# Seven block sums of a Strassen-like second layer, issued one at a time over two steps

## The chip, the core and the metric

One core of a Trainium2 chip runs the whole kernel. The metric is device time in microseconds (us) of one execution. The kernel before was run three times: 1166.24, 1168.34 and 1169.35 us, median 1168.34 us.

The core's engines run side by side and each takes its own instructions in order: TensorE (PE, matmuls; PEld, the loads of its weights), VectorE (DVE), ScalarE (ACT), GpSimd (POOL), and SyncE (SP), which here only issues DMAs. Matmul results land in PSUM, which has eight banks of 128 x 512 float32; everything else lies in SBUF or in DRAM.

## The reference

Chunked attention is followed by two feed-forward layers on 3072 tokens of width 512, with 2048 hidden columns each:

```python
x = attention(q, k, v, mem_k, mem_v)          # (3072, 512)
h = x @ w_in;  x = relu(h) ** 2 @ w_out       # first layer
h = x @ w_in2; g = h * tanh(softplus(h))      # second layer
return g @ w_out2
```

Input and output are float32.

## The kernel before, in words

Each layer works on blocks of 1024 tokens: blocks 0 to 2 belong to the first layer and blocks 3 to 5 to the second. A block takes eight steps, one for each 256 hidden columns, so step s is step s % 8 of block s // 8. Steps 24 to 47 are the second layer's, and the call `step(48)` holds only the end.

Each matrix product is a 2 x 2 block product in Winograd's form: seven products of blocks and of sums of blocks take the place of eight. Each product is made of float32 split into a rounded part and a rest, so that one product of a 256 x 256 by 256 x 512 block takes six matmuls per 128 output rows: high times high, low weight times high, high weight times low.

A step of the second layer does two things in turn. It computes the hidden columns of step s by seven first products, P1, P6, P5, P2, P7, P4, P3 (`product`, line 478), in PSUM banks 0, 1 and 2 (a, b, c). VectorE forms u2, u3, c22, c21 and c12 from them (lines 744, 763, 765, 771, 776), and ScalarE applies the activation (line 501). Between these products it multiplies the hidden columns of step s - 1 with the output weights by seven second products (`product2`, line 568), which I call n0 to n6. Their places in the step are fixed by `wait_point`: P1 P6 n0 P5 n1 P2 n2 P7 n3 n4 P4 P3 n5 n6. Product n takes the block `PRODUCTS2[n][1]`; before, these are B11, B22, B21, T3, T1, T2, T4. Each has two banks: the pairs 4-5 and 6-7 take turns.

The block's operand g is made by `sums_g` (VectorE, line 519: T3, T1, T2, T4), then cast by ScalarE (line 491), then its rest is found by POOL (line 492).

Each second product is added into an SBUF tile m of 128 x 1024 by VectorE (line 556); in a block's first turn, ScalarE copies it there instead (line 579). The tiles of n0, n1 and n2 have tags named by `spare`, ("xt" or "raw") + 0 to 2; the tiles of n3 and n4, and those of n5 and n6, share one buffer each, y0 and y1. A tile of the same tag may be written only when all readers of the one before it have ended.

After the last step of a block, seven sums of the m tiles give its four output blocks (`combine`): T2+=B11, T3+=T2, T2+=T1, T1+=T3, then T4+=T3, B22+=T2, B21+=B11. Each is one VectorE addition of 128 x 1024 with both operands in SBUF, also at line 556. T1, T4, B22 and B21 are then stored (`store_y`). For blocks 3 and 4, the last results come during the first step of the next block (steps 32 and 40), and the first results of the next block during the step after (33 and 41). `done(i)` is called after product n_i and decides which sums stand there. Before, four sums stand after n5 (T2) of steps 32 and 40, and one after each of n0, n1 and n2 of steps 33 and 41.

The last step's hidden columns (step 47) are not multiplied in Winograd's form but by four plain products in step 48 (`last_unit`, line 607), each of 12 matmuls in two banks, added into T4, B21, T1 and B22 and stored. Block 5's sums are made in step 47, ahead of them.

`rest()` is called after each product; there SP issues one load of weights of the step or the next (lines 243 and 245) and the stores that were put off.

Of the kernel before, what the change touches and what calls it, by code (L numbers as in the profile page):

```python
# [25 lines left out]
NQ = KF // 2  # L26
NSB = NT // (2 * NB)
# [9 lines left out]
A22, A11, A12, S1, S2, S3, S4 = range(7)  # L37
B22, B11, B21, T1, T2, T3, T4, B12 = range(8)
P1, P6, P5, P2, P7, P4, P3 = range(7)
PRODUCTS = [(A11, B11), (S2, T2), (S1, T1), (A12, B21), (S3, T3), (A22, T4), (S4, B22)]  # L40

PRODUCTS2 = [(A11, B11), (S4, B22), (A12, B21), (S3, T3), (S1, T1), (S2, T2), (A22, T4)]
STEPS = 2 * NSB * NQ

OUTPUTS = {T4: (1, 0), B21: (0, 0), T1: (1, 1), B22: (0, 1)}
FIRST2 = NSB * NQ
PSB = NP // NSB
POINTS = 15
# [3 lines left out]
def tile_chunk_attention_moe_moe2(  # L52
# [56 lines left out]
    def where(s):  # L109
        return s // (NSB * NQ), s // NQ, s % NQ  # L110
# [165 lines left out]

    def spare(sb, i):

        return f"{('xt', 'raw')[sb % NSB % 2]}{i % 3}"

    def load_apart(sb, o):
        xt_t[sb, o] = pool.tile([128, 2 * NB], FP32, tag=spare(sb - 1, 2 * o), name="xa")
# [189 lines left out]
    def product(s, o, ps, start, stop):  # L472
        wi, xi = PRODUCTS[o]
        w = w1_t[s]
        order = [(kk, a, 0) for kk in range(2) for a in range(2)] + [(kk, 0, 1) for kk in range(2)]
        for i, (kk, a, c) in enumerate(order):
            f = 256 * wi + 128 * kk
            nc.tensor.matmul(  # L478
                out=ps,
                lhsT=w[:, a, f:f + 128],  # L480
                rhs=x[:, xi, c, kk, :],
                start=start and i == 0,
                stop=stop and i == len(order) - 1,
                skip_group_check=True,
            )
# [3 lines left out]
    def split_g(s, key, r):  # L489
        g = g_t[s, key] = new_g(where(s)[0], key)  # L490
        nc.scalar.copy(out=g[:, 0], in_=r)  # L491
        nc.gpsimd.tensor_tensor(out=g[:, 1], in0=r, in1=g[:, 0].bitcast(FP32), op=ALU.subtract)  # L492
# [56 lines left out]
    pairs = [0]  # L549

    def store_y(sb, i, t, y):
        o = 2 * NB * (sb % NSB) + NB * t
        later(out[2 * i:2 * i + 2, :, o:o + NB].rearrange("d p s -> p d s"), y)

    def add(to, in0, in1, engine=nc.vector):
        engine.tensor_tensor(out=to, in0=in0, in1=in1, op=ALU.add)  # L556
# [24 lines left out]
        m = m_t[sb, blk]  # L581
        add(m, ps, m)

    def combine(sb, blk, store):

        m = {b: m_t[sb, b] for _, b in PRODUCTS2}
        if blk == T2:
            add(m[T2], m[T2], m[B11])
            add(m[T3], m[T3], m[T2])
            add(m[T2], m[T2], m[T1])  # L590
            add(m[T1], m[T1], m[T3])
        else:
            add(m[blk], m[blk], m[{T4: T3, B22: T2, B21: B11}[blk]])
        if store:
            store_y(sb, *OUTPUTS[T1 if blk == T2 else blk], m[T1 if blk == T2 else blk])

    def last_unit(s, n):

        sb = where(s)[1]
        blk = list(OUTPUTS)[n]  # L600
        i, t = OUTPUTS[blk]
        first = (4 + 2 * (pairs[0] % 2), 4 + 2 * ((pairs[0] + 1) % 2), 0, 2)[n]
        w = w2_t[s].rearrange("p c (b f) -> p c b f", b=4)
        order = [(f, a, 0) for f in range(2) for a in range(2)] + [(f, 0, 1) for f in range(2)]
        for d in range(2):
            for e, (f, a, c) in enumerate(order):
                nc.tensor.matmul(  # L607
                    out=bank(first + d),
                    lhsT=w[:, a, (2 + f, f)[i], 128 * d:128 * d + 128],
                    rhs=g_t[s, ((B11, B12), (B21, B22))[f][t]][:, c, :],  # L610
                    start=e == 0,
                    stop=e == len(order) - 1,
                )
        m = m_t[sb, blk]
        add(m, banks[:, first:first + 2], m)
        store_y(sb, i, t, m)
        flush()
# [58 lines left out]
    def step(s):  # L676
        live, prev = s < STEPS, s > 0
        layer, sb, j = where(s) if live else (None, None, None)
        point = [0]

        def rest():
            flush()
            i = point[0]
            if NQ <= s + 1 < STEPS and i % 2 == 0 and i < POINTS - 1:
                stream_w(s + 1, 0, i // 2)
            if FIRST2 <= s < STEPS and i % 2 and i // 2 < (7 if s < STEPS - 1 else 4):
                stream_w(s, 1, i // 2)
            if NQ <= s < FIRST2 and i % 3 == 1 and i < 11:
                stream_w(s, 1, i // 3)
            for w in beside.pop((s, point[0]), []):  # L690
                w()
            point[0] += 1

        def units_of(n):
            for i in n:
                if prev:
                    unit(s - 1, i // 4, i % 4, rest)
                else:
                    rest()

        def multiply2(n):
            if prev:
                product2(s - 1, n, rest)
            else:
                rest()

        flush()
        second = s > FIRST2
        if s == FIRST2:
            more["r"] = pool.tile([128, 2, NB], FP32, tag="val", name="more")  # L710

        def wait_point(n):

            if second:
                for i in ((), (0,), (1,), (2,), (3, 4), (5, 6))[n]:
                    product2(s - 1, i, rest)
                    done(i)
            else:
                units_of(((), (), (0, 1), (), (2, 3, 4), (5, 6, 7))[n])

        def done(i):
            _, sb, j = where(s - 1)
            final = s == STEPS - 1
            if (j == NQ - 1 or final) and PRODUCTS2[i][1] == T2:
                combine(sb, T2, not final)
            if final and PRODUCTS2[i][1] == T4:
                for blk in (T4, B22, B21):
                    combine(sb, blk, False)
            if sb > NSB and j == 0 and i < 3:
                combine(sb - 1, (T4, B22, B21)[i], True)  # L730

        if live:
            a, b, c = bank(0), bank(1), bank(2)
            product(s, P1, a, True, False)
            rest()
            u1 = ring("u", 3, [128, NB], FP32, "u1")
            nc.scalar.copy(out=u1, in_=a)  # L737
            if second:
                sums_g(s - 1, T2)
                split_g(s - 1, T3, r_ff[s - 1, T3])  # L740
            product(s, P6, b, True, False)
            rest()
            u2 = ring("u", 3, [128, NB], FP32, "u2")
            nc.vector.tensor_tensor(out=u2, in0=b, in1=u1, op=ALU.add)
            if second:
                sums_g(s - 1, T4)
                split_g(s - 1, T1, r_ff[s - 1, T1])
            wait_point(1)
            product(s, P5, c, True, False)
            rest()  # L750
            if second:
                split_g(s - 1, T2, r_ff[s - 1, T2])
            wait_point(2)
            product(s, P2, a, False, True)
            rest()
            gate(s, 0, 0, a, new_r(layer))
            if second:
                split_g(s - 1, T4, r_ff[s - 1, T4])
            wait_point(3)
            product(s, P7, b, False, False)  # L760
            rest()
            u3 = ring("u", 3, [128, NB], FP32, "u3")
            nc.vector.tensor_tensor(out=u3, in0=b, in1=u1, op=ALU.add)  # L763
            c22 = new_r(layer)
            nc.vector.tensor_tensor(out=c22, in0=c, in1=u3, op=ALU.add)
            gate(s, 1, 1, c22, c22)
            wait_point(4)
            product(s, P4, b, False, True)
            rest()
            c21 = new_r(layer)  # L770
            nc.vector.tensor_tensor(out=c21, in0=b, in1=u1, op=ALU.add)  # L771
            gate(s, 1, 0, c21, c21)
            product(s, P3, c, False, True)
            rest()
            c12 = new_r(layer)
            nc.vector.tensor_tensor(out=c12, in0=c, in1=u2, op=ALU.add)
            gate(s, 0, 1, c12, c12)
            wait_point(5)
            if layer == 1 and s < STEPS - 1:
                sums_g(s, T3)  # L780
                sums_g(s, T1)
        else:
            for n in range(4):
                last_unit(s - 1, n)
        for i in range(POINTS):
            for w in beside.pop((s, i), []):
                w()
        flush()
        if prev and where(s - 1)[0] == 0 and where(s - 1)[2] == NQ - 1:
            sums_y(where(s - 1)[1])  # L790

    with tc.manual_schedule():
# [77 lines left out]
        for n, e in enumerate(seconds):  # L870
            if n < NQ - 2:
                plan_w(NQ + n, 0, e, "Aa|D|d|RS|s|L||||r|l", lambda e, i: round_w2(e, i, "xt2"), split_w2, "val")
            else:
# [4 lines left out]
                    lambda e, i, hi=hi: round_w2(e, i, hi[i]), split_w2, ("val", "at0")[n % 2],  # L878
# [9 lines left out]
        for sb in range(1, 2 * NSB):  # L888
            s = sb * NQ - 1
# [80 lines left out]
```

## Time and profile before

| | |
|---|---|
| three runs | 1166.24, 1168.34, 1169.35 us |
| the profiled execution | 1169.24 us |
| its span, first to last instruction | 1167.2 us |
| TensorE's mean granted clock | 0.972 of full speed |
| busy: PE, DVE, ACT, POOL | 1079.9, 896.1, 561.5, 430.0 us |

All times are counted from the span's start. A row of a timeline gives the start, the duration, the engine, the source line, the operation, what it writes and reads, and how many like instructions in a row it stands for. Brackets hold the idle time just before and what ended it. A row of 12 matmuls that runs on into the next ends, as printed, 0.16 us behind the next one's start, since the end of a matmul is modelled. Where a wait is put down to "issue", the profile shows no other engine that ended it.

The page's chain of waits puts 56% of the span on TensorE and 11% on VectorE. In the second layer, TensorE's rows follow each other without a gap in most steps; they break where a block ends.

### The profile page before, as it was taken

The page shows a single profiled execution, that of the slowest core. Times are in us where ns is not written, and L with a number is a line of the kernel's source. Part 1 is how long each engine was busy: PE and PEld are TensorE (multiplying, and loading weights), DVE is VectorE, ACT ScalarE, POOL GpSimd, SP SyncE. Part 2 cuts the span into 40 slices and gives each one's busy share as a digit, 9 for nine tenths or more (in the row PEclk, how much of TensorE's full clock was granted, in tenths as well). Part 3 has the DMA queues.
Part 4 walks back from the last instruction along what each step waited for, and adds up shares of the span by engine and source line. Part 5 has one row for each costly group of instructions (what it writes and reads, how often), then busy time and mean ns, then how long its engine had stood idle before and what let it go on. Part 6 is the DMA issues. An engine that isn't in the chain of part 4 may idle for free.

```text
span 1167.2 us, 19779 instructions
## 1 busy us (share of the span) xinstructions
PE 1079.9 (93%) x7478; PEld 881.1 (75%) x7478; DVE 896.1 (77%) x1164; ACT 561.5 (48%) x879; POOL 430.0 (37%) x333
## 2 busy tenths in 40 slices
PE   6869899898799889999999999999989999799997
PEld 5748688776677778887777778888868888578885
DVE  5586879969666655678998677898878988768886
ACT  2467555555454444557565645444354443253331
POOL 2423223232223323223222244555355545245451
PEclk9999899999989889999999999999999999899998
DMA  9556867777998786869999958989997889867531
GB/s 359 231 193 233 293 214 262 260 277 248 384 320 315 263 292 241 280 237 395 342 338 329 362 218 289 314 304 339 345 309 276 303 304 391 277 207 230 161 128 72
DMA packets 192125, 324.94 MB, mean 278 GB/s; under 512 B 13344, under 2 KB 151072, under 8 KB 188192
## 3 DMA queue, kind: packets, MB, share of 16 engines
q1 hardware_dynamic: 192032, 323.69, 78.0%
q8 instruction: 60, 0.98, 0.3%
q14 instruction: 33, 0.27, 0.1%
HBM read 231.62 MB, written 92.01 MB: 277 GB/s over the span
## 4 chain that ended last, share of the span: by engine, by line
PE 56%; DVE 11%; DMA 7%; ACT 4%; issue 3%; SPq 0%; DVEq 0%; ACTq 0%
PE banks L478 26%; PE banks L568 17%; PE banks L533 10%; DMA w_d<-hi 2%; DVE m L556 2%; DVE y L547 1%; PE banks L414 1%; PE banks L607 1%; DMA w1s<-w_d 1%; DVE ty L632 1%; DVE val L152 1%; DVE r L519 1%; ACT r L497 1%; DMA xt<-xt_d 1%; DMA w2s<-w_d 1%
## 5 line engine op out<-in xcount | busy, mean ns | idle before, releaser
L478 PE MATMUL banks<-x,w1s 128*128 128x512 f32 x2016 | 507.8, 399 | 23.5 <-DVE u L763 7.5
L492 POOL TENSOR_TENSOR g<-r,g 128x512 fp32r<-128x512 f32 x206 | 287.3, 1401 | 537.5 <-ACT g L491 442.6
L478 PEld LDWEIGHTS banks<-x,w1s 128*128 128x128 f32 x2016 | 385.8, 193 | 112.5 <-DVE u L763 9.7
L533 PE MATMUL banks<-g,w2s 128*128 128x512 f32 x1152 | 282.4, 395 | 6.8 <-DVE y L547 5.3
L533 PEld LDWEIGHTS banks<-g,w2s 128*128 128x128 f32 x1152 | 217.2, 190 | 57.7 <-DVE y L547 8.2
L568 PE MATMUL banks<-g,w2s 128*128 128x512 f32 x966 | 241.3, 392 | 9.8 <-ACT m L579 7.6
L568 PEld LDWEIGHTS banks<-g,w2s 128*128 128x128 f32 x966 | 181.2, 189 | 52.2 <-ACT m L579 9.7
L556 DVE TENSOR_TENSOR m<-banks,m 128x1024 f32<-128x1024 f32 x144 | 173.6, 1218 | 34.9 <-PE banks L568 26.3
L491 ACT CAST g<-r 128x512 fp32r<-128x512 f32 x206 | 127.0, 621 | 37.5 <-DVE r L519 30.3
L547 DVE TENSOR_TENSOR y<-banks,y 128x512 f32<-128x512 f32 x168 | 112.0, 682 | 39.0 <-PE banks L533 38.9
L492 POOL TENSOR_TENSOR g<-more,g 128x512 fp32r<-128x512 f32 x55 | 79.7, 1453 | 81.0 <-ACT g L491 66.6
L497 ACT ACTIVATE r<-r 128x512 f32<-128x512 f32 x72 | 45.4, 631 | 69.7 <-DVE r L771 50.1
L501 ACT ACTIVATE r<-r 128x512 f32<-128x512 f32 x48 | 30.4, 632 | 71.4 <-DVE r L771 35.9
L211 ACT CAST hi<-val 128x1024 fp32r<-128x1024 f32 (+1 forms) x32 | 30.4, 949 | 69.5 <-DVE val L156 50.5
L498 ACT ACTIVATE r<-r 128x512 f32<-128x512 f32 x96 | 60.7, 632 | 3.1
L152 DVE TENSOR_SCALAR val<-val 128x512 f32<-128x512 f32 x64 | 38.9, 607 | 26.5 <-ACT val L145 26.4
L414 PE MATMUL banks<-pt,v 64*64 64x32 f32 x1536 | 39.9, 262 | 19.4 <-ACT pt L402 19.0
L218 DVE TENSOR_TENSOR val<-val,hi 128x1024 f32<-128x1024 f32 (+1 forms) x32 | 37.2, 1162 | 25.2 <-ACT hi L211 25.0
L414 PEld LDWEIGHTS banks<-pt,v 64*64 64x64 f32 x1536 | 37.0, 185 | 25.7 <-ACT pt L402 24.8
L737 ACT COPY u<-banks 128x512 f32<-128x512 f32 x48 | 28.1, 585 | 52.0 <-PE banks L478 52.0
L384 POOL TENSOR_TENSOR p<-p,sum 128x512 f32<-128x512 f32 x24 | 28.7, 1215 | 63.3 <-DVE sum L381 25.0
L344 PE MATMUL banks<-k,q 64*32 64x64 f32 x1536 | 37.5, 250 | 13.2 <-DMA k<-k_dram 7.1
(71 smaller groups left out, 999.9 us busy)
## 6 DMA issues: line engine op xcount, KB each, us to landing
w1s<-w_d SPq DMA_DIRECT2D x280, 256.0 KB, 5.4
w2s<-w_d SPq DMA_DIRECT2D x229, 256.0 KB, 5.3
raw<-w_dram SPq DMA_DIRECT2D x64, 512.0 KB, 5.0
w_d<-w1s SPq DMA_DIRECT2D x8, 1792.0 KB, 7.5
x<-xs_d SPq DMA_DIRECT2D x14, 1024.0 KB, 10.7
k<-k_dram SPq DMA_DIRECT2D x24, 512.0 KB, 7.0
v<-v_dram SPq DMA_DIRECT2D x24, 512.0 KB, 8.9
xt<-xt_d SPq DMA_DIRECT2D x21, 512.0 KB, 7.3
```

What stands on the lines that cost most here:

```text
L152: nc.vector.tensor_scalar(out=val, in0=val, scalar1=LIMIT, scalar2=-LIMIT * NEGATIVE, op0=ALU.min, op1=ALU.max)
L344: nc.tensor.matmul(out=s4[32 * c:32 * c + 32, j, hp, :], lhsT=q_t[p][r0:r0 + 64, j, hp, 32 * c:32 * c + 32], rhs=k_t[p][r0:r0 + 64, j, hp, ...
L414: nc.tensor.matmul(out=x_ps[par][64 * h2:64 * h2 + 64, o:o + 32], lhsT=v_t[p][j][r0:r0 + 64, h2, a, c, :], rhs=pt_t[p][r0:r0 + 64, h2, j, ...
L478: nc.tensor.matmul(out=ps, lhsT=w[:, a, f:f + 128], rhs=x[:, xi, c, kk, :], start=start and i == 0, stop=stop and i == len(order) - 1, ski ...
L491: nc.scalar.copy(out=g[:, 0], in_=r)
L492: nc.gpsimd.tensor_tensor(out=g[:, 1], in0=r, in1=g[:, 0].bitcast(FP32), op=ALU.subtract)
L497: nc.scalar.activation(out=r, in_=h, func=ACTF.Relu)
L498: nc.scalar.activation(out=r, in_=r, func=ACTF.Square)
L533: nc.tensor.matmul(out=ps, lhsT=w[:, a, blk(f), d % 2 * 128:d % 2 * 128 + 128], rhs=g_t[s, (f, t)][:, c, :], start=i == 0, stop=i == len(o ...
L547: nc.vector.tensor_tensor(out=y, in0=ps, in1=y, op=ALU.add)
L556: engine.tensor_tensor(out=to, in0=in0, in1=in1, op=ALU.add)
L568: nc.tensor.matmul(out=bank(first + d), lhsT=w[:, a, 128 * d:128 * d + 128], rhs=g[:, c, :], start=i == 0, stop=i == 2)
```

## The change

Four things change. `PRODUCTS2` swaps T1 and T2, so n4 is T2 and n5 is T1, and with it the pairs that share a buffer: T3 and T2 in y0, T1 and T4 in y1. The seven sums become a list, `SUMS`, and `done` issues them one by one: T2+=B11 after n4 and T3+=T2 after n5 of the block's last products; T2+=T1 ahead of P6 of the step after; T1+=T3, T4+=T3, B22+=T2 and B21+=B11 after n0, n1, n2 and n3 of it, the last four with a store each. In step 47 the first stands after n4, three after n5 and three after n6. `spare` takes turns from block 3 on: the fifth block's first three tiles are tagged raw and not xt, as the fourth's are. Last, `last_unit` begins in banks 0-1 and 2-3 and then takes the two pairs.

```diff
-PRODUCTS2 = [(A11, B11), (S4, B22), (A12, B21), (S3, T3), (S1, T1), (S2, T2), (A22, T4)]
+PRODUCTS2 = [(A11, B11), (S4, B22), (A12, B21), (S3, T3), (S2, T2), (S1, T1), (A22, T4)]
+SUMS = [(T2, B11), (T3, T2), (T2, T1), (T1, T3), (T4, T3), (B22, T2), (B21, B11)]
...
-        return f"{('xt', 'raw')[sb % NSB % 2]}{i % 3}"
+        return f"{('xt', 'raw')[(sb - NSB) % 2]}{i % 3}"
...
-    def combine(sb, blk, store):
+    def combine(sb, to, other, store=False):
         m = {b: m_t[sb, b] for _, b in PRODUCTS2}
-        if blk == T2:
-            add(m[T2], m[T2], m[B11])
-            add(m[T3], m[T3], m[T2])
-            add(m[T2], m[T2], m[T1])
-            add(m[T1], m[T1], m[T3])
-        else:
-            add(m[blk], m[blk], m[{T4: T3, B22: T2, B21: B11}[blk]])
-        if store:
-            store_y(sb, *OUTPUTS[T1 if blk == T2 else blk], m[T1 if blk == T2 else blk])
+        add(m[to], m[to], m[other])
+        if store and (to, other) in SUMS[3:]:
+            store_y(sb, *OUTPUTS[to], m[to])
...
-        first = (4 + 2 * (pairs[0] % 2), 4 + 2 * ((pairs[0] + 1) % 2), 0, 2)[n]
+        first = (0, 2, 4 + 2 * (pairs[0] % 2), 4 + 2 * ((pairs[0] + 1) % 2))[n]
...
         def done(i):
             _, sb, j = where(s - 1)
-            final = s == STEPS - 1
-            if (j == NQ - 1 or final) and PRODUCTS2[i][1] == T2:
-                combine(sb, T2, not final)
-            if final and PRODUCTS2[i][1] == T4:
-                for blk in (T4, B22, B21):
-                    combine(sb, blk, False)
-            if sb > NSB and j == 0 and i < 3:
-                combine(sb - 1, (T4, B22, B21)[i], True)
+            blk = PRODUCTS2[i][1]
+            if s == STEPS - 1:
+                for n in {T2: (0,), T1: (1, 2, 3), T4: (4, 6, 5)}.get(blk, ()):
+                    combine(sb, *SUMS[n])
+            elif j == NQ - 1:
+                for n in {T2: (0,), T1: (1,)}.get(blk, ()):
+                    combine(sb, *SUMS[n])
+            elif sb > NSB and j == 0:
+                for n in {B11: (3,), B22: (4,), B21: (5,), T3: (6,)}.get(blk, ()):
+                    combine(sb - 1, *SUMS[n], store=True)
...
                 split_g(s - 1, T3, r_ff[s - 1, T3])
+                if where(s - 1)[1] > NSB and where(s - 1)[2] == 0:
+                    combine(where(s - 1)[1] - 1, *SUMS[2])
             product(s, P6, b, True, False)
```

The first place is VectorE from n5's addition in step 32 to u3 in step 33. Before, m_6714 is the buffer of T2 and T4, m_6673 that of T3 and T1, and m_6606, m_6625 and m_6649 are B11, B22 and B21:

```order
L556 TENSOR_TENSOR m_6714<-banks_70,m_6714 128x1024
L556 TENSOR_TENSOR m_6714<-m_6714,m_6606 128x1024
L556 TENSOR_TENSOR m_6673<-m_6673,m_6714 128x1024
L556 TENSOR_TENSOR m_6714<-m_6714,m_6673 128x1024
L556 TENSOR_TENSOR m_6673<-m_6673 128x1024
L556 TENSOR_TENSOR m_6714<-banks_70,m_6714 128x1024
...
L744 TENSOR_TENSOR u2_7855<-banks_70,u1_7841 128x512
L519 TENSOR_TENSOR r_7793<-r_7793,r_7763 128x512
L556 TENSOR_TENSOR m_6714<-m_6714,m_6673 128x1024
L556 TENSOR_TENSOR m_6625<-m_6625,m_6714 128x1024
L556 TENSOR_TENSOR m_6649<-m_6649,m_6606 128x1024
L763 TENSOR_TENSOR u3_7925<-banks_70,u1_7841 128x512
```

In the changed kernel m_6673 is the buffer of T3 and T2 and m_6714 that of T1 and T4. The same stretch, again from n5's addition to u3:

```order
L558 TENSOR_TENSOR m_6714<-banks_70,m_6714 128x1024
L558 TENSOR_TENSOR m_6673<-m_6673 128x1024
L558 TENSOR_TENSOR m_6714<-banks_70,m_6714 128x1024
L521 TENSOR_TENSOR r_7827<-r_7763,r_7807 128x512
L521 TENSOR_TENSOR r_7807<-r_7807,more_6412 128x512
L521 TENSOR_TENSOR r_7763<-r_7763,r_7807 128x512
L558 TENSOR_TENSOR m_6673<-m_6673,m_6714 128x1024
L744 TENSOR_TENSOR u2_7853<-banks_70,u1_7838 128x512
L521 TENSOR_TENSOR r_7794<-r_7794,r_7763 128x512
L558 TENSOR_TENSOR m_6714<-m_6714,m_6673 128x1024 x2
L558 TENSOR_TENSOR m_6625<-m_6625,m_6673 128x1024
L763 TENSOR_TENSOR u3_7923<-banks_70,u1_7838 128x512
```

One sum in place of four now stands between the additions of n5 and n6, one stands ahead of u2, and three stand between u2 and u3 as before. T2+=B11 stands ahead of c21 of step 32, and B21+=B11 behind c22 of step 33.

The second place is ScalarE at the copies of n0 and n1 in step 41, with what each instruction waits for. Before:

```order
L737 COPY u_9107<-banks 128x512 [waits PE_49]
L491 CAST g<-r 128x512 [waits DVE_49] x2
L579 COPY m<-banks 128x1024 [waits DVE_49,PE_49]
L491 CAST g<-more 128x512
L579 COPY m<-banks 128x1024 [waits DMAHW1_49,PE_49]
```

In the changed kernel:

```order
L735 COPY u_9104<-banks 128x512 [waits PE_49]
L493 CAST g<-r 128x512 [waits DVE_49] x2
L581 COPY m<-banks 128x1024 [waits DMAHW2_49,DMAHW0_49,PE_49]
L493 CAST g<-more 128x512 [waits DVE_49]
L581 COPY m<-banks 128x1024 [waits DMAHW1_49,PE_49]
```

The copy of n0 waits for VectorE before, and for two DMAs in the changed kernel.

The third place is TensorE at the first two plain products, with waits. Before:

```order
L607 MATMUL banks<-g,w2s 128x512 [waits DMAHW2_49,DVE_49]
L607 MATMUL banks<-g,w2s 128x512
L607 MATMUL banks<-g,w2s 128x512 [waits DMAHW3_49,Activation_49]
L607 MATMUL banks<-g,w2s 128x512 x2
L607 MATMUL banks<-g,w2s 128x512 [waits Pool_49]
L607 MATMUL banks<-g,w2s 128x512 x6
L607 MATMUL banks<-g,w2s 128x512 [waits DMAHW4_49,DVE_49]
```

In the changed kernel:

```order
L603 MATMUL banks<-g,w2s 128x512 [waits DMAHW2_49]
L603 MATMUL banks<-g,w2s 128x512
L603 MATMUL banks<-g,w2s 128x512 [waits DMAHW3_49,Activation_49]
L603 MATMUL banks<-g,w2s 128x512 x2
L603 MATMUL banks<-g,w2s 128x512 [waits Pool_49]
L603 MATMUL banks<-g,w2s 128x512 [waits DVE_49]
L603 MATMUL banks<-g,w2s 128x512 x5
L603 MATMUL banks<-g,w2s 128x512 [waits DMAHW4_49,DVE_49]
```

The first matmul no longer waits for VectorE; the waits that stand further on are for VectorE's reads of banks 1 and 2 in step 47 instead of the additions of n5 and n6.

## Rows read from the trace of the kernel before

**Rows 1.** The page: the span, then busy time by engine

```profile
span 1167.2 us, 19779 instructions
PE 1079.9 (93%) x7478; PEld 881.1 (75%) x7478; DVE 896.1 (77%) x1164; ACT 561.5 (48%) x879; POOL 430.0 (37%) x333
```

**Rows 2.** Timeline of TensorE, steps 32 to 42: start us, us, what

```profile
821.08 2.88 PE L478 MATMUL banks<-x,w1s 128*128 128x512 f32 x12
...
840.12 2.88 PE L478 MATMUL banks<-x,w1s 128*128 128x512 f32 x12
...
846.46 1.62 PE L568 MATMUL banks<-g,w2s 128*128 128x512 f32 x6 [0.74 <-issue]
...
858.62 4.50 PE L478 MATMUL banks<-x,w1s 128*128 128x512 f32 x12 [3.17 <-DVE u L763]
...
865.80 2.88 PE L478 MATMUL banks<-x,w1s 128*128 128x512 f32 x12
...
1000.19 2.88 PE L478 MATMUL banks<-x,w1s 128*128 128x512 f32 x12
...
1015.89 2.93 PE L568 MATMUL banks<-g,w2s 128*128 128x512 f32 x6 [6.36 <-ACT m L579]
...
1029.98 2.88 PE L478 MATMUL banks<-x,w1s 128*128 128x512 f32 x12
```

**Rows 3.** Timeline of all engines, end of step 47 and step 48

```profile
1141.50 2.88 PE L568 MATMUL banks<-g,w2s 128*128 128x512 f32 x12
...
1143.06 1.22 DVE L556 TENSOR_TENSOR m<-banks,m 128x1024 f32<-128x1024 f32 x1 [0.60 <-PE banks L568]
...
1144.32 5.72 DVE L556 TENSOR_TENSOR m<-m 128x1024 f32<-128x1024 f32 x4
...
1151.24 11.04 PE L607 MATMUL banks<-g,w2s 128*128 128x512 f32 x36 [3.84 <-DVE m L556]
...
1162.32 1.23 DVE L556 TENSOR_TENSOR m<-banks,m 128x1024 f32<-128x1024 f32 x1 [1.49 <-PE banks L607]
```

**Rows 4.** Timeline of all engines, end of step 32 and step 33

```profile
835.03 1.29 POOL L492 TENSOR_TENSOR g<-r,g 128x512 fp32r<-128x512 f32 x1 [1.66 <-ACT g L491]
...
836.31 0.69 DVE L771 TENSOR_TENSOR r<-banks,u 128x512 f32<-128x512 f32 x1 [0.21 <-PE banks L478]
...
838.96 1.22 DVE L556 TENSOR_TENSOR m<-banks,m 128x1024 f32<-128x1024 f32 x1 [0.60 <-PE banks L568]
...
840.22 5.01 DVE L556 TENSOR_TENSOR m<-m 128x1024 f32<-128x1024 f32 x4
...
845.25 0.40 SPq L129 DMA_DIRECT2D out_dram<-m  x1
...
851.22 6.74 DVE L556 TENSOR_TENSOR m<-m 128x1024 f32<-128x1024 f32 x3
...
852.44 2.24 POOL L492 TENSOR_TENSOR g<-more,g 128x512 fp32r<-128x512 f32 x1
...
857.89 0.68 DVE L763 TENSOR_TENSOR u<-banks,u 128x512 f32<-128x512 f32 x1
```

**Rows 5.** Busy by engine, granted clock, DMA share, GB/s in slices of 1 us

```profile
860.00:861.00 1.00, 1.00 (x4) 0.81 (x3) 0.33 (x1) 0.96 (x2) 0.26 (x1) 0.50 1.04 371
...
1157.00:1158.00 1.00, 1.00 (x6) 0.82 (x5) 0.99 (x1) 0.00 (x0) 0.00 (x0) 1.00 1.06 412
```

**Rows 6.** Timeline of TensorE, first layer, around 626 us

```profile
626.52 4.50 PE L478 MATMUL banks<-x,w1s 128*128 128x512 f32 x12 [2.22 <-ACT u L737]
```

**Rows 7.** Timeline of all engines, step 41

```profile
1011.25 3.48 DVE L556 TENSOR_TENSOR m<-m 128x1024 f32<-128x1024 f32 x3
...
1014.83 1.01 ACT L579 COPY m<-banks 128x1024 f32<-128x1024 f32 x1 [6.41 <-DVE m L556]
```

**Rows 8.** Timeline of all engines, step 25: T2's low half on POOL, then n4

```profile
695.30 1.63 POOL L492 TENSOR_TENSOR g<-r,g 128x512 fp32r<-128x512 f32 x1 [3.55 <-ACT g L491]
...
698.83 1.65 PE L568 MATMUL banks<-g,w2s 128*128 128x512 f32 x6 [0.55 <-ACT m L579]
```

## The prediction

> **What bounds the kernel now.** I read the page first, then TensorE alone in order of time for the second layer, then all engines around the two places where its period broke, then the last 30 us. The page says that TensorE is busy for 93% of 1167.2 us [rows 1]; the profiled execution took 1169.24 us, so 2.04 us lie outside the span, and the median of the three runs, 1168.34 us, is 0.90 us below it. TensorE's rows show why 93% is not the whole story. A step of the second layer starts with P1, and a quiet step lasts 840.12 - 821.08 = 19.04 us, which is 84 matmuls back to back (14 products of 1.36 us). Nothing can be gained in such a step without fewer matmuls. Two steps are longer: step 33 lasts 865.80 - 840.12 = 25.68 us and step 41 lasts 1029.98 - 1000.19 = 29.79 us [rows 2]. They lose 6.64 and 10.75 us. The third place is the end: TensorE waits 3.84 us ahead of the second plain product, and the last addition ends at 1163.55, 3.6 us before the span does [rows 3]. The seven block sums lie in front of all three.
>
> **Step 33, before.** VectorE's queue from the addition of product n5 (838.96) to u3 (857.89) holds seven sums: four in 5.01 us, 1.25 each, and three in 6.74 us, 2.25 each. The three run beside a POOL that is working without a pause, and its subtractions last 2.24 us instead of 1.29 there: the two engines take turns, so that a sum with both operands in SBUF costs one pass of POOL more. u3 reads the bank that P4 writes, so P4 waits, 3.17 us [rows 2, 4]. After the wait the granted clock is 0.50, its lower level of 1.2 GHz [rows 5]: from P4 to the next P1 it takes 865.80 - 858.62 = 7.18 us instead of 4 x 1.36 = 5.44.
>
> **Step 33, after.** Five sums are left between that addition and u3: T2+=B11 moves in front of c21, and B21+=B11 behind c22. I price them so: T3+=T2 at 1.65 (1.25 and part of one POOL pass, since POOL's pass for B21 comes about 1 us later and meets it), T2+=T1, T1+=T3 and T4+=T3 at 2.25 each beside POOL's passes for T3, T1, T2, B11 and T4, and B22+=T2 at 1.25, since POOL has nothing more to do until c22. That is 9.65 us against 5.01 + 6.74 = 11.75: u3 and P4 come 2.1 us earlier. P4 then starts at about 856.5 and is due at 840.12 + 10 x 1.36 = 853.72, so 2.8 us of waiting stay. The small waits ahead of it (0.74 at n1 [rows 2]) go too, but they lie in front of the same u3 and give nothing of their own. Bounds: five sums at 1.25 are 6.25, 5.5 us less than before, which leaves u3 in time and gives back the whole 6.64; five at 2.25 are 11.25, only 0.5 less. I take 2.1, since POOL's passes of this stretch are the same in number as before.
>
> A wait of 2.8 us lies between two whose cost is seen: the row of 12 matmuls behind a wait of 2.22 us lasts 4.50 us, as long as the one behind 3.17 us, where quiet rows of 12 last 2.88 [rows 2, 6]. So I leave the loss at the lower clock in: 7.18 - 5.44 = 1.74 us, of which the gain takes nothing.
>
> The covers: T2+=B11 delays c21 from 836.31 to about 837.4, and c21's bank is wanted by the next P6 only, at 840.12 + 1.36 = 841.5; the delay is used up in VectorE's idle times, 0.21 ahead of c21 and 0.60 ahead of n5's addition [rows 4]. B21+=B11 runs while TensorE is in P4 and c21 cannot start. If that cover were gone, each would cost 1.25 us at most.
>
> **Step 41** has the same work and one thing more: ScalarE's copy of n0 waits 6.41 us, until the three sums have ended (1011.25 + 3.48 = 1014.73) [rows 7], because the new block's first three results lie in the very tiles that hold the old block's. TensorE waits 6.36 us for that copy [rows 2]. In the changed kernel the fourth block's results lie in the xt tiles and the fifth's in the raw tiles, and the order shows this copy waiting for two DMAs and the product, as in step 33. So step 41 becomes what step 33 becomes, 25.68 - 2.1 = 23.6 us, and gains 29.79 - 23.6 = 6.2. Bounds: 4.6 if step 33 gains its least, 10.75 if its most.
>
> **The end.** Before, the second plain product takes the bank pair that n6 left, whose addition stands behind four sums: TensorE stops until 1151.24, and its 36 matmuls then take 11.04 us instead of 36 x 0.227 = 8.2 [rows 3]. After, the first two plain products go into banks 0 to 3. Bank 3 is idle, banks 0 and 1 were read before n5 began, and bank 2 is read by c12 ahead of n5's addition, two units before the second plain product wants it. So TensorE runs through from 1141.50 + 2.72 = 1144.2 and ends at 1144.2 + 4 x 2.72 = 1155.1. Then VectorE sets the end. From n5's addition at 1143.06 it has six additions out of banks (n5, n6, four plain products; 1.22 and a gap, 1.24) and six sums (1.25): 14.9 us, and two passes of POOL in its way, 0.6 for the rest of the first and 1.0 for the second (a sum beside POOL costs 2.25 - 1.25 = 1.0 more; before, the four sums paid 5.72 - 5.01 = 0.7 in all [rows 3, 4]). That is 1159.6. The last addition ends at 1162.32 + 1.23 = 1163.55 before, so the gain is 3.95. The four stores then follow each other at 1.24 us instead of some 2.7. 524 KB at 412 GB/s, the rate of a full slice with a store in it, last 1.27 us [rows 5]; with starting and ending I estimate 1.4 each, so the last finds 3 x 0.15 = 0.4 us of others in front of it. That leaves 3.55. Bounds: 2.6 if the stores' queue costs 1.4, 5.6 if POOL is never in the way.
>
> **What costs nothing.** The swap of T1 and T2 asks for T2's halves one product (1.36 us) earlier in each of 23 steps. The tightest is step 25: POOL ends that pass at 695.30 + 1.63 = 696.93, and the product that would use it starts at 698.83 [rows 8]. That wait of 0.55 is for ScalarE's copy; without it the product would start at 698.1, still 1.2 us behind POOL, and only its third matmul wants that half. The bounds are zero and, were the pass late by a whole product, 1.36 us in step 25. That two tiles hold other pairs of blocks changes which addition frees them, and each is freed before it is wanted.
>
> **Sum:** 2.1 + 6.2 + 3.55 = 11.85 us. 1169.24 - 11.85 = 1157.4 for an execution like the profiled one, and 1168.34 - 11.85 = 1156.5 for the median, which I predict.
>
> **Rivals.**
> (1) The clock stays up after the shorter wait. Then 1.7 us more come back in each of the two steps: 1156.5 - 3.4 = 1153.1. For it: waits of 0.74 left the clock alone [rows 2]. Against it: 2.22 did not. The Trainium skill, "TensorE: Matmul & The Clock Gate", section "Why this matters for your kernels", advises to keep idle gaps between bursts short, since a long enough one sends the array back to half rate. By that rule a gap that is cut short enough pays twice, and it would give this rival's time; the trace agrees in both its halves (0.74 kept the clock, 2.22 lost it) and puts our 2.8 on the wrong side.
> (2) All five sums pay a pass of POOL. The moves then buy 0.5 in step 33, 4.6 in step 41 and 3.55 at the end, 8.65: 1159.7. For it: all three that ran beside POOL did pay [rows 4]. Against it: POOL has no pass left for the last. The Trainium skill, "SBUF — State Buffer", section "SBUF: two separate sides", calls the pair of ports that the two engines share an exclusive lock held for a whole instruction, with the loser fully blocked. By that rule a sum spread out into POOL's work is a worse sum, which speaks against the change and for this rival; the trace agrees with 2.25 against 1.25 us.
> (3) The sums get out of POOL's way altogether: 6.64 + 10.75 + 3.55 = 20.9, 1147.4. The fewer delays ahead speak for it, the same count of POOL passes against it.
> (4) The tiles don't come free as I think, and step 41 keeps its collision: it gains 2.1 like step 33, and the sum is 7.75: 1160.6. The order shows the wait gone, so little speaks for it.
> (5) A wait of the same size takes the place of u3, and nothing is gained: 1168.
> (6) Slower: SP issues the weights in order, and the first store now waits for T1+=T3, to about 852.5 (u3 at 857.89 - 2.1 = 855.8, less 1.25 and 2.25, rounded up), instead of 845.25 [rows 4]. With it go 12 loads and three more stores. At 412 GB/s a load of 256 KB lasts 0.64 us and a store 1.27 [rows 5], so the queue is empty at about 852.5 + 12 x 0.64 + 4 x 1.27 = 865.3. The loads come in the order in which the next step uses them, and each has some 12 us in hand (the third product's weights are there at about 855, and the next P5 wants them at 863.7 + 3 x 1.36 = 867.8). It decides only from a queue 12 us later than this; at 20 us it costs 8 in each of the two steps: 1156.5 + 16 = 1172.5.
>
> **How the numbers follow.** Chances: forecast 0.62 (its own range 1154.5 to 1158.5), rival 1 0.13, rival 2 0.12, rival 3 0.05, rival 4 0.02, rival 5 0.03, rival 6 0.03. The range 1152 to 1161 takes in the forecast and rivals 1, 2 and 4 and leaves out 0.11. About 0.3%, 3.5 us, is what a measurement of this kernel tells from no change. The first four rivals and the forecast are faster by more, 0.94; rival 5 is the same, 0.03; rival 6 is slower, 0.03.
>
> **What would show it.** In the profile after: steps 33 and 41 of equal length, near 23.6 us; P4 waiting for u3 nearly 3 us in both and the clock at 0.50 behind it; no copy of n0 that waits for VectorE; no wait of TensorE among the plain products, and VectorE without a gap from n5's addition to the end. I am wrong if either step differs from 23.6 by over 1.5 us, if the plain products wait, or if a quiet step is not 19.04 us.

## The result, and the profile after

Four runs of the changed kernel took 1148.02 to 1154.43 us, median 1150.85. The kernel before has four runs of 1166.01 to 1169.35 beside it, median 1167.29; three of them are those that the prediction started from. The ratio is 0.9859 [0.9824, 0.9894]. The forecast was 1156.5, its range 1152 to 1161: the direction was right, but the gain was larger than forecast and the median lies below the range.

The profiled execution took 1149.29 us. The page answers to [rows 1]:

```profile
span 1147.5 us, 19757 instructions
PE 1070.4 (93%) x7478; PEld 875.6 (76%) x7478; DVE 899.6 (78%) x1164; ACT 561.5 (49%) x879; POOL 432.0 (38%) x333
```

TensorE has the same 7478 matmuls and VectorE the same 1164 instructions. TensorE's share of 93% has not moved although 19.7 us of the span are gone: the share says nothing of the waits that went.

TensorE's timeline of the second layer, for [rows 2]:

```profile
678.52 2.88 PE L480 MATMUL banks<-x,w1s 128*128 128x512 f32 x12
...
833.58 2.88 PE L480 MATMUL banks<-x,w1s 128*128 128x512 f32 x12
...
839.02 1.52 PE L570 MATMUL banks<-g,w2s 128*128 128x512 f32 x6
...
849.87 4.41 PE L480 MATMUL banks<-x,w1s 128*128 128x512 f32 x12 [2.53 <-DVE u L763]
...
857.06 2.88 PE L480 MATMUL banks<-x,w1s 128*128 128x512 f32 x12
...
991.30 2.88 PE L480 MATMUL banks<-x,w1s 128*128 128x512 f32 x12
...
999.46 1.52 PE L570 MATMUL banks<-g,w2s 128*128 128x512 f32 x6
...
1007.57 4.61 PE L480 MATMUL banks<-x,w1s 128*128 128x512 f32 x12 [2.50 <-DVE u L763]
...
1014.76 2.88 PE L480 MATMUL banks<-x,w1s 128*128 128x512 f32 x12
...
1129.00 11.04 PE L603 MATMUL banks<-g,w2s 128*128 128x512 f32 x48
```

The starts of P1 give the lengths: step 33 lasts 857.06 - 833.58 = 23.48 us and step 41 lasts 23.46, where 23.6 was forecast for both. The product n2 of step 41, which takes the banks that n0's copy reads, starts at 999.46 without a wait (6.36 before), and n1 of step 33 at 839.02 without one (0.74 before). One wait is left in each of the two steps: P4 for u3, 2.5 us. The last line is the end: 48 plain matmuls in 11.04 us, no wait among them.

ScalarE's copy of n0 in step 41, for [rows 7], follows the instruction ahead of it without idle time, where it waited 6.41 us for VectorE before:

```profile
996.02 1.01 ACT L581 COPY m<-banks 128x1024 f32<-128x1024 f32 x1
```

The clock behind P4's wait is at its lower level of 1.2 GHz again, as in [rows 5] (the third number from the right is the granted clock):

```profile
852.00:853.00 1.00, 1.00 (x4) 0.80 (x3) 0.52 (x1) 1.00 (x2) 1.00 (x1) 0.50 0.97 325
```

All engines, the end of step 32 and step 33, for [rows 4]:

```profile
829.60 1.27 DVE L558 TENSOR_TENSOR m<-m 128x1024 f32<-128x1024 f32 x1
830.79 0.68 DVE L771 TENSOR_TENSOR r<-banks,u 128x512 f32<-128x512 f32 x1
...
833.57 1.75 DVE L558 TENSOR_TENSOR m<-m 128x1024 f32<-128x1024 f32 x1
...
839.60 2.31 DVE L558 TENSOR_TENSOR m<-m 128x1024 f32<-128x1024 f32 x1
...
843.54 5.67 DVE L558 TENSOR_TENSOR m<-m 128x1024 f32<-128x1024 f32 x3
...
849.14 0.68 DVE L763 TENSOR_TENSOR u<-banks,u 128x512 f32<-128x512 f32 x1
...
850.46 1.22 DVE L558 TENSOR_TENSOR m<-m 128x1024 f32<-128x1024 f32 x1
```

The seven sums are there one by one. The five between n5's addition and u3 take 1.75 + 2.31 + 5.67 = 9.73 us; the forecast had 9.65. The first and the last of the seven, outside that stretch, take 1.27 and 1.22.

All engines, the end, for [rows 3]:

```profile
1127.84 1.22 DVE L558 TENSOR_TENSOR m<-banks,m 128x1024 f32<-128x1024 f32 x1 [0.36 <-PE banks L570]
...
1128.98 5.21 DVE L558 TENSOR_TENSOR m<-m 128x1024 f32<-128x1024 f32 x3
...
1134.12 1.22 DVE L558 TENSOR_TENSOR m<-banks,m 128x1024 f32<-128x1024 f32 x1
1135.37 3.50 DVE L558 TENSOR_TENSOR m<-m 128x1024 f32<-128x1024 f32 x3
1138.78 4.61 DVE L558 TENSOR_TENSOR m<-banks,m 128x1024 f32<-128x1024 f32 x4
```

VectorE has no gap from n5's addition to the last one, which ends at 1143.39; 4.1 us later the span ends.

From the start of step 25 to the span's end the profiled execution before has 1167.2 - 685.01 = 482.2 us, and the one after 1147.5 - 678.52 = 469.0. So 13.2 of the 19.7 us come from where the change is, and 6.5 from steps 0 to 24, which hold the same instructions in both kernels. That split is what the first and last experiments are about.

### The profile page after: what moved, and what is told of

It reads as the page before. It is cut to its first block, busy times and chain, and to the rows that moved or that the text cites. A ratio compares the mean times of both kernels' runs of the same rounds, so it can differ in the third digit from the quotient of the medians.

```text
span 1147.5 us, 19757 instructions
## 1 busy us (share of the span) xinstructions
PE 1070.4 (93%) x7478; PEld 875.6 (76%) x7478; DVE 899.6 (78%) x1164; ACT 561.5 (49%) x879; POOL 432.0 (38%) x333
## 4 chain that ended last, share of the span: by engine, by line
PE 53%; DVE 12%; DMA 8%; issue 4%; ACT 4%; SPq 0%; POOL 0%; DVEq 0%; ACTq 0%
PE banks L480 24%; PE banks L570 16%; PE banks L535 10%; DVE m L558 3%; DMA w_d<-hi 3%; DMA w2s<-w_d 2%; DVE y L549 1%; PE banks L416 1%; DVE r L521 1%; DMA w1s<-w_d 1%; DVE ty L628 1%; DMA xt_d<-stage 1%; PE banks L346 1%; DVE val L158 1%; DVE val L154 1%
## 5 line engine op out<-in xcount | busy, mean ns | idle before, releaser
L154 DVE TENSOR_SCALAR val<-val 128x512 f32<-128x512 f32 x64 | 38.5, 602 | 25.7 <-ACT val L147 25.6
L416 PE MATMUL banks<-pt,v 64*64 64x32 f32 x1536 | 37.4, 253 | 17.4 <-ACT pt L404 16.8
L416 PEld LDWEIGHTS banks<-pt,v 64*64 64x64 f32 x1536 | 34.5, 174 | 23.6 <-ACT pt L404 22.3
L158 DVE SCALAR_TENSOR_TENSOR val<-raw,val 128x512 uint32<-128x512 uint32 x64 | 48.9, 764 | 2.2
```

The lines of the kernel that those rows point to most:

```text
L154: nc.vector.tensor_scalar(out=val, in0=val, scalar1=LIMIT, scalar2=-LIMIT * NEGATIVE, op0=ALU.min, op1=ALU.max)
L158: nc.vector.scalar_tensor_tensor(out=vb, in0=low, scalar=29, in1=vb, op0=ALU.logical_shift_right, op1=ALU.bitwise_or)
L416: nc.tensor.matmul(out=x_ps[par][64 * h2:64 * h2 + 64, o:o + 32], lhsT=v_t[p][j][r0:r0 + 64, h2, a, c, :], rhs=pt_t[p][r0:r0 + 64, h2, j, ...
```

## The experiments

Two theories are to be told apart. Theory A is the prediction's mechanism, with the early 6.5 us as a difference between executions that both kernels show. Theory B is that the changed program also has a shorter early part of its own.

**The kernel before, again, and the changed kernel, again (no edit).**

> The kernel before, unchanged. In the two traces the steps ahead of step 25, in which both programs hold the same instructions, differ by 6.5 us (P1 of step 25 starts at 685.0 before and 678.5 after). Theory A (those 6.5 us are the executions' own, since the first layer's steps hang on when DMAs land): ratio 1.000 within 0.2%, and P1 of step 25 starts anywhere from 678 to 690. Theory B (the changed program shifts the early steps too): ratio 1.000 as well, but P1 of step 25 stays within 1.5 us of 685.

> The changed kernel, unchanged. The rows of steps 25 to 48 give 2.2 us in step 33, 6.3 in step 41 and 4.5 at the end, 13.2 with the small change in the steps between. Theory A: -13 to -14 us, ratio 0.988 to 0.989, and P1 of step 25 not where it was (678.5). Theory B: -16 us or more again, ratio 0.986 or less, P1 of step 25 within 1.5 us of 678.5.

> The changed kernel again, beside e5 to e8. P1 of step 25 started at 685.0 and 681.5 in two profiled executions of the kernel before and at 678.5 and 678.8 in two of the changed one, but at 678.0 and 675.1 in those of e3 and e4. Theory A (chance of the execution): P1 of step 25 starts at another place in 675 to 686, and the time falls by 12.5 to 14 us, ratio 0.988 to 0.989. Theory B (the changed program starts the second layer 3 us earlier): 678 to 679 again, and -15 to -16 us, ratio 0.986 to 0.987.

The kernel before took 1165.64 us in 12 runs (1161.25 to 1168.26), and 29 more runs of it on that chip have the median 1165.66 and reach from 1158.2 to 1169.61. The three runs that the prediction started from, median 1168.34, lie in the upper part of that. The changed kernel took 1149.72 (ratio 0.9873 [0.9846, 0.9901]) and, on another chip, 1150.98 (0.9885 [0.9861, 0.9909]). Three profiled executions of the changed kernel agree within 0.1 us from step 25 on, and put that step's start at 678.52, 678.79 and 678.93; the second of the kernel before puts it at 681.51, not 685.01. In the last of these runs the start at 678.93 spoke for B and the ratio of 0.9885 for A. These were too few to part A from B.

**Where step 25 starts, in four more executions (no edit).**

> The kernel before, one more profiled execution. Where does P1 of step 25 start? So far 685.01 and 681.51 us in it, 678.52, 678.79 and 678.93 in the changed kernel, though steps 0 to 24 hold the same instructions in both. Theory A (early parts vary from execution to execution, alike in both kernels): the four new executions, two of each kernel, overlap, with means within 1.5 us. Theory B (the changed program has a shorter early part of its own): before 681 to 685 again, changed 678 to 679.5 again, means 3 us or more apart. Steps 33 and 41 and the end stay at 25.6, 29.8 and 41 to 42 by both.

> The changed kernel, one more profiled execution, for the same question. A: P1 of step 25 anywhere from 675 to 685. B: 678 to 679.5. Steps 33 and 41 and the end stay at 23.5, 23.4 and 37.5 by both.

> The kernel before, a second look of this kind. A: P1 of step 25 anywhere from 675 to 685; B: 681 to 685.

> The changed kernel, a second look of this kind. A: P1 of step 25 anywhere from 675 to 685; B: 678 to 679.5.

The four starts were 680.27 and 679.07 in the kernel before, 675.52 and 683.72 in the changed one: means 679.67 and 679.62. B as it was put, with the changed kernel held to 678 to 679.5, is refuted: its executions spread as widely as those of the kernel before. Over all nine executions the means are 681.5 before and 679.1 after, 2.4 apart, where the starts of one kernel spread over 5.9 and of the other over 8.2 us, so a shift smaller than B's is not excluded. The spread is made of many small steps in the first layer and the attention beside it. One of them is step 11, in TensorE's timeline of the two executions of the changed kernel, here the early one:

```profile
352.67 4.42 PE L480 MATMUL banks<-x,w1s 128*128 128x512 f32 x18
...
375.39 0.30 PE L416 MATMUL banks<-pt,v 64*64 64x32 f32 x2 [2.45 <-ACT pt L404]
375.88 2.88 PE L416 MATMUL banks<-pt,v 64*64 64x32 f32 x126 [0.19 <-ACT pt L404]
378.69 2.35 PE L535 MATMUL banks<-g,w2s 128*128 128x512 f32 x6
```

and here the late one:

```profile
357.45 4.42 PE L480 MATMUL banks<-x,w1s 128*128 128x512 f32 x18
...
381.06 0.30 PE L416 MATMUL banks<-pt,v 64*64 64x32 f32 x2 [3.35 <-ACT pt L404]
381.55 3.63 PE L416 MATMUL banks<-pt,v 64*64 64x32 f32 x126 [0.19 <-ACT pt L404]
385.11 2.93 PE L535 MATMUL banks<-g,w2s 128*128 128x512 f32 x6
```

One wait is 0.9 us longer, and the same 126 + 6 matmuls behind it take 1.3 us longer: 2.2 of the 8.2 us between the two starts. What makes the wait longer was not traced further.

The downstream part, step 25 to the end, is now known from four executions of the kernel before (482.2, 480.8, 483.5, 483.0, mean 482.4) and five of the changed one (469.0, 469.0, 469.0, 469.2, 469.2, mean 469.1). The change is worth 13.3 us there. Its parts by the means: step 33 26.2 to 23.5 (-2.7), step 41 29.75 to 23.4 (-6.3), the end 41.8 to 37.55 (-4.3).

**The order of banks alone**, in the kernel before:

```diff
-        first = (4 + 2 * (pairs[0] % 2), 4 + 2 * ((pairs[0] + 1) % 2), 0, 2)[n]
+        first = (0, 2, 4 + 2 * (pairs[0] % 2), 4 + 2 * ((pairs[0] + 1) % 2))[n]
```

> The kernel before, and only the plain products begin in banks 0 to 3. Theory A: TensorE runs through the 48 matmuls in about 11 us, VectorE then sets the end with its 13 operations in a row from n5's addition; from P1 of step 47 to the end 42.0 becomes 38 to 39 us, and the time falls by 3 to 4 us. Theory B: the same end, but the early steps fall by 3 to 6 us more as in any other program: -6 to -10 us.

It took 1161.96 us in 12 runs, ratio 0.9971 [0.9953, 0.9989], which is 3.4 us less. Steps 33 and 41 keep 25.7 and 29.8; the end falls to 38.19. All engines at the end:

```profile
1137.10 11.04 PE L607 MATMUL banks<-g,w2s 128*128 128x512 f32 x48
1137.20 5.75 DVE L556 TENSOR_TENSOR m<-m 128x1024 f32<-128x1024 f32 x4
```

Four sums still stand in front of n6's addition, and TensorE runs past them. So the bank order alone gives 3.6 of the 4.3 us at the end.

**The tiles alone**, in the kernel before:

```diff
-        return f"{('xt', 'raw')[sb % NSB % 2]}{i % 3}"
+        return f"{('xt', 'raw')[(sb - NSB) % 2]}{i % 3}"
```

> The kernel before, and only the fifth block's first three results go to the raw tiles. Theory A: step 41 becomes as long as step 33, 25.7 us instead of 29.8, all else stays, and the time falls by 4 us. Rival: step 41 stays near 29.8, since the three sums and not the copy hold it: no change. Theory B: -7 to -10 us, with the early steps shorter too.

It took 1160.16 us in 12 runs, ratio 0.9951 [0.9937, 0.9966], which is 5.7 us less; by the profile, step 41 falls from 29.8 to 25.64. The collision with n0's copy was the tiles', worth 4.1 us with the sums where they were. Its execution also shows P4's wait in steps 33 and 41, in TensorE's timeline:

```profile
848.72 3.02 PE L478 MATMUL banks<-x,w1s 128*128 128x512 f32 x12 [3.15 <-DVE u L763]
...
1007.42 4.58 PE L478 MATMUL banks<-x,w1s 128*128 128x512 f32 x12 [3.15 <-DVE u L763]
```

The same wait of 3.15 us cost nothing behind it in one step and 1.6 us in the other.

The new order of sums with the old tiles was not tried: there n0's copy would have to wait for a sum that stands behind c22, and c22 itself comes after that copy, so neither could start.

**The old bank order in the changed kernel**: the bank edit above, reversed.

> The changed kernel, but the plain products take their banks as before: the two pairs first. TensorE waits some 3.6 us ahead of the second plain product, for n6's addition behind three sums, then runs at the lower clock: from P1 of step 47 to the end 42 us instead of 37.5, and the time is 4.4 us above the changed kernel. Rival (spreading the sums alone frees the banks in time): 37.5 to 38.5.

It took 1152.04 us, ratio 0.9901 [0.9874, 0.9929], beside 0.9885 [0.9861, 0.9909] for the changed kernel in the same session: the times don't part them. By the profiles the end is 38.79 against 37.55, not the 42 that was expected of it. TensorE's timeline shows why:

```profile
1136.35 8.46 PE L603 MATMUL banks<-g,w2s 128*128 128x512 f32 x36 [3.20 <-DVE m L558]
```

TensorE does wait, 3.20 us, but the 36 matmuls behind take 8.46 us instead of 11.04 [rows 3]: three sums in place of four stood in front, and in this execution the clock was kept. The bank order and the spread sums are two ways to the same microseconds; with the sums spread, the banks add 1.2, and with the banks free, the spread sums add 38.19 - 37.55 = 0.6. Each of these ends is read from one execution.

**The swap of T1 and T2 undone**, so that T2+=B11 stands behind n5:

```diff
-PRODUCTS2 = [(A11, B11), (S4, B22), (A12, B21), (S3, T3), (S2, T2), (S1, T1), (A22, T4)]
+PRODUCTS2 = [(A11, B11), (S4, B22), (A12, B21), (S3, T3), (S1, T1), (S2, T2), (A22, T4)]
...
-                for n in {T2: (0,), T1: (1, 2, 3), T4: (4, 6, 5)}.get(blk, ()):
+                for n in {T2: (0, 1, 2, 3), T4: (4, 6, 5)}.get(blk, ()):
...
-                for n in {T2: (0,), T1: (1,)}.get(blk, ()):
+                for n in {T2: (0, 1)}.get(blk, ()):
```

> The changed kernel with T1 as n4 and T2 as n5, as before: T2+=B11 then stands behind n5 with T3+=T2 (in step 47 with T2+=T1 and T1+=T3 too). If the swap is worth one sum's time in front of u3 and of the end: steps 33 and 41 take 24.7 us instead of 23.5, the end 1.2 more than 37.5, and the time is 3 to 4 us above the changed kernel, 9 to 10 below the one before. Rival (the sum is hidden there too): all three as in the changed kernel.

It took 1153.8 us, ratio 0.9906 [0.9882, 0.9929]: 2.8 above the changed kernel, with intervals that overlap. By the profiles step 33 is longer by 0.8, step 41 shorter by 0.4 and the end longer by 0.7, 1.1 in all, less than the 3 to 4 expected. TensorE's timeline, P4 in steps 33 and 41:

```profile
853.73 4.60 PE L480 MATMUL banks<-x,w1s 128*128 128x512 f32 x12 [2.90 <-DVE u L763]
...
1012.35 3.02 PE L480 MATMUL banks<-x,w1s 128*128 128x512 f32 x12 [2.88 <-DVE u L763]
```

P4 waits 0.4 us longer than in the changed kernel. The clock was lost in step 33 and kept in step 41 of this execution; had the row cost 4.60 us in step 41 too, the three would make 2.7 and not 1.1. So the swap gives something, but how much these runs don't settle.

**Two of the three sums moved behind u3.** If P4's remaining 2.5 us are the three sums between u2 and u3, moving two of them out gives them back:

```diff
-                for n in {B11: (3,), B22: (4,), B21: (5,), T3: (6,)}.get(blk, ()):
+                for n in {B11: (3,), T3: (4, 5), T2: (6,)}.get(blk, ()):
```

> The changed kernel, but of the three sums that stood between u2 and u3 of steps 33 and 41 only T1+=T3 stays there; T4+=T3 and B22+=T2 follow n3, behind c22, and B21+=B11 follows n4. Theory A (P4 waits for u3, and u3 for the sums in front of it, each 2.25 us beside POOL): u3 comes some 3.5 us earlier and P4 no longer waits; n5 then waits for the copy of n3, which waits for the two sums, 1.2 us or less, too short to lose the clock. Steps 33 and 41 become about 20.3 us instead of 23.5, and the time falls by about 6 us against the changed kernel, 19 against the one before. Rival (u3 is late by the additions and the subtractions ahead of it, or P4 waits for a weight load): both steps stay near 23.5. Rival 2: ScalarE, held by n3's copy, makes c21's activation late and costs the 3 us again.

It took 1146.87 us in 6 runs (1141.28 to 1150.46), ratio 0.984 [0.981, 0.9871], against 1150.98 for the changed kernel beside it: the lowest median of all versions, though the two intervals overlap a little. Steps 33 and 34 together last 40.52 us instead of 42.53, steps 41 and 42 39.99 instead of 42.50: 4.5 us in all. TensorE's timeline of steps 33 and 34:

```profile
852.53 2.88 PE L480 MATMUL banks<-x,w1s 128*128 128x512 f32 x12
855.96 3.01 PE L570 MATMUL banks<-g,w2s 128*128 128x512 f32 x12 [0.54 <-ACT m L581]
858.81 2.88 PE L480 MATMUL banks<-x,w1s 128*128 128x512 f32 x12
863.00 1.65 PE L570 MATMUL banks<-g,w2s 128*128 128x512 f32 x6 [1.31 <-ACT m L581]
```

and ScalarE's of the same stretch:

```profile
854.89 1.93 ACT L581 COPY m<-banks 128x1024 f32<-128x1024 f32 x2 [0.98 <-DVE m L558]
...
861.93 1.93 ACT L581 COPY m<-banks 128x1024 f32<-128x1024 f32 x2 [2.46 <-PE banks L480]
```

P4 (852.53) no longer waits and the clock stays up. The sums that moved hold up something else: n3's and n4's copies wait for them, as those tiles share a buffer with the old T3 and T2, and n5 waits 0.54 for the copies. Then the copies of n5 and n6 start only at 861.93, and n0 of the next step waits 1.31 for them. The view names TensorE as what held them; it had been done earlier, and for the same copies of step 41 the profile names no engine at all. Their tile holds the old block's T1 and T4, and SP's queue has the store of T4 only among the two at 856.39, 5.5 us ahead of the copy:

```profile
851.24 0.39 SPq L131 DMA_DIRECT2D out_dram<-m  x1
...
856.39 1.06 SPq L131 DMA_DIRECT2D out_dram<-m  x2
```

The landing times agree: the first of these two stores lands 5.5 us after its issue, at 861.9, and the copies start at 861.93; in step 41 it lands 5.7 us after 1011.34, at 1017.0, and the copies start at 1017.07. So the copies wait for that store; no run moves it. Steps 33 and 41 themselves became shorter by 3.6 us each, more than the 3.2 expected, and the steps behind them gave back 1.6 and 1.1.

## Why the prediction was wrong, point by point

**The mechanism held.** Steps 33 and 41 came out equal, within 0.2 us of the 23.6 forecast. P4 waited 2.53 and 2.50 us (2.8 forecast) with the clock at 0.50 behind it, quiet steps kept their 19.04 us, n0's copy did not wait for VectorE, the plain products ran through, and VectorE set the end. By the prices: T3+=T2 took 1.75 (1.65), T2+=T1 2.31 (2.25), and the three after it 5.67 (5.75).

**Step 33** was forecast at -2.1 and gave -2.2 between the first two profiles. Against four executions of the kernel before it is -2.7, since its step 33 lasted 25.5 to 26.95 us: the 12 matmuls behind the same wait of 3.17 us took 4.50 us in [rows 2] and, in TensorE's timeline of another execution of the kernel before, 5.49:

```profile
853.82 5.49 PE L478 MATMUL banks<-x,w1s 128*128 128x512 f32 x12 [3.17 <-DVE u L763]
```

**Step 41** gave -6.3; -6.2 was forecast.

**The end** was mis-sized: -3.55 forecast, -4.45 between the first two profiles. The terms were 1.24 or 1.25 us for each of VectorE's twelve last instructions, and POOL's two passes at 1.6. From n5's addition to the end of the last that made 16.54 us; it took 1143.39 - 1127.84 = 15.55. The last seven run beside an idle POOL and wait for nothing: three sums in 3.50 us and four additions in 4.61, about 1.16 each, which is 0.7 of the 1.0 us. In the kernel before, the last additions of the end waited for TensorE, so the pace could not be read from them; but [rows 7] shows it, three sums in 3.48 us beside an idle POOL, 1.16 each. The forecast took 1.25 from the four sums of [rows 4], where each has a tile in common with the one ahead of it. The three sums beside POOL took 5.21, where 3 x 1.25 + 1.6 = 5.35 was forecast. From the last addition to the span's end it takes 4.1 us, against 3.6 [rows 3]: the stores' queue cost 0.5, with 0.4 forecast.

**The step that failed** is the last, "1168.34 - 11.85 = 1156.5 for the median", with the range set around it. It took three runs for the kernel's level and one execution's first 25 steps as fixed, so the sum has no term for what differs between executions of the same instructions. The runs showed 6.5 us there between the first two profiles, and starts of step 25 from 675.52 to 685.01 in nine executions. The terms of the change were mis-sized by less: it is worth 13.3 us and not 11.85, an error of 1.5 (0.6 of it in step 33, 0.75 at the end, 0.1 in step 41), and 1168.34 - 13.3 = 1155.0 would still have been in the range.

The level was off: the kernel before has the median 1165.66 over 29 runs on one chip and 1164.2 over 11 on another, 2.7 and 4.1 below 1168.34. With the first of them the prediction's own 11.85 gives 1153.8, and 13.3 gives 1152.4. The median of four runs, 1150.85, is 1.5 below that, inside a spread of executions that reaches over 11 us in 29 runs of one kernel. How much of the miss is the level and how much the chance of four runs is not settled: from the 1167.29 beside the result, 13.3 gives 1154.0, 3.1 above it. The range of 1152 to 1161 was made of the change's bounds alone; nothing in it stood for this spread, and it had to.

**The rivals.** (1), the clock stays up, would have given 1153.1, near the measured time, and yet it is not what happened: all five profiled executions of the changed kernel have both steps at 23.4 to 23.5 us. A time that agrees is no proof of its mechanism. (2) was wrong: the three sums behind u2 took 5.67 us, which is two at 2.25 and one at 1.17, so that one of the five is clear of POOL, and T3+=T2 (1.75) paid half a pass. (3) to (5) did not occur. (6) did not either: TensorE waits for no weights in steps 33, 34, 41 and 42.

**Still open:** what lengthens single waits of the first layer from one execution to the next, and why some waits of about 3 us lose the clock and others keep it.

## What to carry to other kernels

Split a measured difference at the last point up to which both kernels hold the same instructions: what lies behind it belongs to the change, and here it took nine profiled executions to see that the other 6.5 of 19.7 us are within what executions of one kernel differ by. A range needs a term for the spread of executions beside the bounds of the change's own costs, and three runs don't show that spread. Two edits that relieve the same wait (here the bank order and the spread sums) don't add up: alone they took 3.6 us (41.8 to 38.19) and 3.0 us (to 38.79) off the end, together 4.3. Price the second with the first in place.

## What the runs showed of the hardware that was not expected

The same wait of TensorE keeps or loses the clock. Behind 3.15 us, 12 matmuls took 3.02 us in step 33 and 4.58 in step 41 of one execution; behind 2.90 and 2.88 us 4.60 and 3.02; behind 3.17 us 4.50 and 5.49 in two executions of one kernel. In [rows 6] 2.22 us lost it, and 3.20 us at the end kept it (36 matmuls in 8.46 us). In the changed kernel, though, all ten rows behind P4's wait of 2.50 to 2.53 us were slow, 4.41 to 4.61 us. So a single row behind a wait does not price the next one: the forecast's 1.74 us came from one row and held for the changed kernel, while the same row of the kernel before took up to 1.0 us more in other executions.

VectorE's additions of 128 x 1024 that have no tile in common with their neighbours follow each other at some 1.16 us (3.50 for three, 4.61 for four, and 3.48 for three in [rows 7]) when POOL is idle and nothing is waited for, though a single one is shown with 1.22 to 1.27 us. The four sums of [rows 4], each with a tile in common with the one ahead, take 5.01 us beside an idle POOL, 1.25 each. That the common tile makes the difference is what these rows suggest; no run varies it alone.
